# Weight conversions cut in halves and laid on half units, two of them taken into the opening steps, and the last weight's sums spread over ten units

## The chip, the cores and the metric

The kernel runs on one core of one Trainium2 chip. The metric is device microseconds of one execution; the time given for a kernel is the median of its runs. The engines are named as in the profile: PE (TensorE matmul), DVE (VectorE), ACT (ScalarE), POOL (GpSimd), SP (SyncE, which here issues nearly all DMAs).

## The reference, cut to what matters

Sparse attention, then two feed-forward blocks, all in float32, with float64 weights that the kernel turns into pairs of float32 parts on the chip.

```python
# q_l, k_l, v_l: 4 x 8 heads x 512 x 64 ; q_g, k_g, v_g: 4 x 8 x 32 x 64
s_g = scale * q_g @ [k_g, k_l]^T ;  out_g = softmax(s_g) @ [v_g, v_l]        # global rows
s_l = scale * q_l @ [k_g, k_l inside a window of 32 on both sides]^T
out_l = softmax(s_l) @ [v_g, v_l]
x = [out_g, out_l], heads side by side        # 2176 tokens x 512
h = x @ w_in                                  # 512 x 2048
g = where(h >= 1, h, where(h <= -1, 0, (h + 1)**2 / 4))
x = g @ w_out                                 # 2048 x 512
out = (x @ w_a * (x @ w_b)) @ w2_out          # 512 x 1536, 512 x 1536, 1536 x 512
```

## The kernel before

**Tiles and units.** Tokens are cut into six tiles (TILES), mostly of three blocks of 128 tokens, 384 columns wide. The first feed-forward block runs per tile in 16 units f, one for each slice of 128 of the 2048 hidden columns. A unit has two halves. The first (`h_unit`, kind 0) makes 12 matmuls into the PSUM tile hp (lines 593 to 595: each float32 product is three, high part by high, low by high, high by low); then ACT forms r (L921), DVE m (L922, L923), and one unit later ACT and DVE split m into g's high and low part (L926, L927). The second half (`x_unit`, kind 1) makes 12 matmuls of g of two units earlier (LAG) with w_out into four PSUM banks acc. PSUM tiles of tag "h" share four banks: hp, the attention's scores s, its transposes tp, its products o, ot.

**Order of the tiles.** `stages` says: tile 0's units 0 to 5, tile 1's 16 units, tile 0's units 6 to 15, then tiles 2 to 5. The attention of the next tile (its 12 items in 4 groups: s, masks L219, exps L227, transposes, o, os, ot) is cut into atoms that are dealt out between the halves. The attention of tile 0 itself runs before all this, in `begin()`, four steps k with filler matmuls (warm), whose order on each engine is fixed as written (`in_order`).

**Conversions.** The float64 weights of the first block come as 32 slices of 512 KB (i0, i1, o0, i2, o1, ...; `ws1`). Each is loaded to a raw tile (L102), and converted: ACT L110 reads the high words, DVE L111 and L112 put in the low words (`w_conv`), then ACT L119 and DVE L120 split the float32 into a high and a low part (`split`). The first ten raw tiles have buffers of their own; after that there are two (`sp["raw"]`), so a load waits until the L112 of two conversions earlier has read its tile. Before, i0 is converted in `begin()`'s steps 2 and 3, and i1 after the last step, followed by the masks and exps of tile 1's first group. Then a whole conversion at a time (`W1.step`) is issued ahead of a unit: in tile 0's units two a unit, in tile 1's one or two a unit until unit 12, each behind the newest L921 and L923 (`paced`).

**Second block.** Tiles go in three pairs (PAIRS) through 12 units of seven products (`ab_unit`, with y products L849 to L851). `side(u)` hangs other work on its places k: the next pair's sums (`x_pre`, L652 and L653) and splits (`x_op`), and during the second pair the sums of w2_out (`yw_sum`: four additions yq, L764 to L767; `yw_split`: two splits yo, L120), of which there are six. The third pair runs in `ab_step`.

The scheduler of the language layer decides the final order on each engine from the order in which the code issues, the dependencies and the `issue_after` edges; every engine then works its own list strictly in order.

Of the kernel before, what the change touches and what calls it, by code (L numbers as in the profile page):

```python
# [14 lines left out]
ALU = mybir.AluOpType  # L15
# [38 lines left out]
LEAD1 = 2  # L54
# [15 lines left out]
def body(tc, qk, vw, kg, vg, vt, w1i, w1o, w2a, w2b, w2o, mask, eye, out):  # L70
# [404 lines left out]
    pend = []  # L475
# [6 lines left out]
    def w_end():  # L482
        key, tf = pend.pop(0)
        w = slot()
        split(w[:, 0], w[:, 1], tf)
        wslots[key] = w

# [15 lines left out]
    def begin():  # L503
# [9 lines left out]
        for k in range(n):  # L513
# [5 lines left out]
            if k == n - 1:  # L519
                w_end()  # L520
            fill(FILLS[0])
            v_part(g[k])
            s_part(g[k + 2]) if k + 2 <= n else None
            g[k].v_post()
            if k + 2 < n:
                g[k + 2].mask()
            elif k + 2 == n:
                w_begin()
            fill(FILLS[1])
# [4 lines left out]
        w_begin()  # L534
        g[n].s_post()
# [361 lines left out]
    def paced(fn):  # L897

        with tc.issue_after(at["act"]), tc.issue_after(at["dve"]):
            return fn()  # L900

    def h_unit(t, f):
# [22 lines left out]
        def fin():  # L925
            nc.scalar.activation(gh[:, :W], m[:, :W], AF.Copy)  # L926
            nc.vector.tensor_tensor(gl[:, :W], m[:, :W], f32(gh[:, :W]), ALU.subtract)  # L927
# [41 lines left out]
    for u in range(len(units)):  # L969
        for kind in (0, 1):  # L970
            if kind == 0:
                if u >= len(units):
                    continue
                t, f = units[u]
                si = stage[u]
                if si == 0:
                    while f and W1.si < min(2 * f + LEAD1, n1):
                        paced(W1.step)
                if si == 1:
                    want = max(n1 + (len(ws1) - n1) * (f + 1) // (NF1 - 3), 2 * f + LEAD1 + 2)  # L980
                    while W1.si < min(want, len(ws1)):
                        paced(W1.step)
                if si == 1 and f == NF1 - 3:
# [64 lines left out]

    def side(u):
# [7 lines left out]
        def run(k):  # L1057
            if f == 1 and k == 0:
                x1_load(s + 1)
            if f == NF2 - 2 and k == 6:  # L1060
                behind(x_pre, s + 1)
# [11 lines left out]
            if s == 1:  # L1073
                c = f // 2
                if f % 2 == 0:
                    if k == 0 and f == 0:
                        yw_load(0)
                    elif k == 6:
                        behind(yw_sum, c)
                        if c < 5:  # L1080
                            yw_load(c + 1)
                elif k in (2, 5):
                    yw_split(c, k // 3)
# [256 lines left out]
```

## Time and profile before

| | |
|---|---|
| Runs of the kernel before | 897.07, 897.57, 901.92 us; median 897.57 us |
| The profiled execution's own time | 897.45 us |
| Its span in the profile | 895.6 us |
| PE busy | 874.0 us, 98% of the span |
| DVE busy | 621.0 us, 69% |
| ACT busy | 474.7 us, 53% |
| Granted TensorE clock, mean of the span | 0.994 |

The profile is of one execution. Its time is 1.85 us longer than its span, and 0.12 us below the median of the runs. A row of a timeline is "start us, duration us, engine, line, operation, out<-in, shape, count", and in square brackets how long the engine sat idle before it and what ended that. Durations of matmuls overlap: the step from one to the next is the rate. PEclk is the granted TensorE clock as a share of 2.4 GHz, so 1.00 is 2.4 GHz and a stretch wholly at 1.2 GHz reads 0.50.

### The profile page before, as it was taken

How to read it: one execution, taken by the hardware profiler on the slowest of the kernel's cores; microseconds unless marked ns; L12 is line 12 of the kernel's file. 1: busy time of each engine (PE TensorE's matmuls, PEld its weight loads, DVE VectorE, ACT ScalarE, POOL GpSimd, SP SyncE). 2: the span in 40 equal slices, each digit the busy share in tenths (PEclk: the TensorE clock that was granted, in tenths of full speed). 3: DMA queues.
4: the chain of work that ended last, by engine and by line, in shares of the span. 5: the costliest groups of instructions: out<-in, count | busy, mean ns of one | idle time of the engine just before them, and what ended most of it. 6: DMA issues, size and time to landing. Idle time of an engine off the chain costs nothing.

```text
span 895.6 us, 19345 instructions
## 1 busy us (share of the span) xinstructions
PE 874.0 (98%) x7394; PEld 822.9 (92%) x7394; DVE 621.0 (69%) x1524; ACT 474.7 (53%) x1151; POOL 0.3 (0%) x5
## 2 busy tenths in 40 slices
PE   7899989999999999999999999999999999999998
PEld 6688979999999999988999999999999998999998
DVE  4888887676556555555498687777977769776683
ACT  4787664555445444434465555555645556455442
POOL 0000000000000000000000000000000000000000
PEclk9999989999999999999999999999999999999999
DMA  9977664875344532444373455433486532644521
GB/s 312 387 216 241 211 220 140 277 228 187 119 149 139 165 135 89 137 127 133 118 241 113 150 171 165 164 118 121 135 303 220 188 129 91 198 140 130 192 110 53
DMA packets 77612, 153.60 MB, mean 172 GB/s; under 512 B 9296, under 2 KB 35792, under 8 KB 77520
## 3 DMA queue, kind: packets, MB, share of 16 engines
q1 hardware_dynamic: 76944, 151.85, 51.6%
q8 instruction: 58, 0.95, 0.4%
q10 hardware_dynamic: 576, 0.52, 0.2%
q14 instruction: 34, 0.28, 0.1%
HBM read 119.05 MB, written 33.29 MB: 170 GB/s over the span
## 4 chain that ended last, share of the span: by engine, by line
PE 83%; DMA 9%; DVE 4%; ACT 3%; issue 1%; SPq 1%; ACTq 0%; DVEq 0%
PE hp L593 6%; PE acc L593 6%; PE hp L595 6%; PE acc L594 6%; PE hp L594 6%; PE acc L595 6%; PE pb L785 4%; PE pb L783 4%; PE pb L786 4%; PE py L850 3%; PE py L851 3%; PE py L849 3%; PE px L783 3%; DMA wraw<-in_w1i_dram 3%; PE px L786 3%; PE px L785 3%
## 5 line engine op out<-in xcount | busy, mean ns | idle before, releaser
L593 PE MATMUL hp<-xh,w 128*128 128x384 f32 (+1 forms) x384 | 132.2, 344 | 4.4 <-DVE m L922 3.0
L593 PE MATMUL acc<-g,w 128*128 128x384 f32 (+1 forms) x384 | 127.8, 334 | 0.8 <-ACT w L119 0.8
L594 PE MATMUL hp<-xh,w 128*128 128x384 f32 (+1 forms) x384 | 127.2, 331 | 0.1
L595 PE MATMUL hp<-xl,w 128*128 128x384 f32 (+1 forms) x384 | 127.2, 332 | 0.0
L595 PE MATMUL acc<-g,w 128*128 128x384 f32 (+1 forms) x384 | 126.3, 329 | 0.0
L594 PE MATMUL acc<-g,w 128*128 128x384 f32 (+1 forms) x384 | 125.9, 328 | 0.0
L922 DVE SCALAR_TENSOR_TENSOR m<-hp,r 128x384 f32<-128x384 f32 (+1 forms) x96 | 51.2, 533 | 69.3 <-ACT r L921 68.5
L921 ACT ACTIVATE r<-hp,half 128x384 f32<-128x384 f32 (+1 forms) x96 | 53.8, 560 | 79.5 <-PE hp L595 78.6
L926 ACT ACTIVATE g<-m 128x384 fp32r<-128x384 f32 (+1 forms) x96 | 48.7, 507 | 61.3 <-DVE m L923 61.0
L593 PEld LDWEIGHTS hp<-xh,w 128*128 128x128 f32 x384 | 73.4, 191 | 6.9 <-DVE m L922 3.1
L783 PE MATMUL pb<-w 128*128 128x384 f32 (+1 forms) x240 | 78.1, 325 | 0.4 <-DVE m L827 0.2
L785 PE MATMUL pb<-w 128*128 128x384 f32 (+1 forms) x240 | 78.2, 326 | 0.0
L786 PE MATMUL pb<-w 128*128 128x384 f32 (+1 forms) x240 | 78.0, 325 | 0.0
L119 ACT ACTIVATE w<-wt 128x512 fp32r<-128x512 f32 (+1 forms) x94 | 53.2, 572 | 43.8 <-PE pb L786 30.6
L593 PEld LDWEIGHTS acc<-g,w 128*128 128x128 f32 x384 | 72.7, 190 | 2.0 <-ACT w L119 1.0
L595 PEld LDWEIGHTS hp<-xl,w 128*128 128x128 f32 x384 | 73.4, 191 | 1.0 <-DMA xl<-x0d 0.6
L594 PEld LDWEIGHTS hp<-xh,w 128*128 128x128 f32 x384 | 73.5, 191 | 0.7 <-DVE w L120 0.5
L595 PEld LDWEIGHTS acc<-g,w 128*128 128x128 f32 x384 | 72.6, 189 | 0.5 <-DVE g L927 0.2
L594 PEld LDWEIGHTS acc<-g,w 128*128 128x128 f32 x384 | 72.8, 190 | 0.1
L927 DVE TENSOR_TENSOR g<-m,g 128x384 fp32r<-128x384 f32 (+1 forms) x96 | 51.1, 533 | 23.0 <-ACT g L926 22.5
L227 ACT ACTIVATE e<-e,mn 128x128 f32<-128x128 f32 x128 | 48.0, 395 | 26.0 <-DVE os L261 22.6
L120 DVE TENSOR_TENSOR w<-wt,w 128x512 fp32r<-128x512 f32 (+1 forms) x94 | 57.5, 616 | 4.1 <-ACT w L119 3.1
(171 smaller groups left out, 2001.3 us busy)
## 6 DMA issues: line engine op xcount, KB each, us to landing
v<-in_vw_dram SPq DMA_DIRECT2D x64, 256.0 KB, 4.9
wt<-wd SPq DMA_DIRECT2D x50, 256.0 KB, 2.9
qk<-in_qk_dram SPq DMA_DIRECT2D x62, 176.0 KB, 4.5
wraw<-in_w1i_dram SPq DMA_DIRECT2D x16, 512.0 KB, 5.2
wraw<-in_w1o_dram SPq DMA_DIRECT2D x16, 512.0 KB, 4.1
wraw<-in_w2a_dram SPq DMA_DIRECT2D x12, 512.0 KB, 3.7
wraw<-in_w2b_dram SPq DMA_DIRECT2D x12, 512.0 KB, 3.7
wd<-wt SPq DMA_DIRECT2D x24, 256.0 KB, 2.2
```

Of the source, the lines that this page charges most:

```text
L119: nc.scalar.activation(hi, src, AF.Copy)
L120: nc.vector.tensor_tensor(lo, src, f32(hi), ALU.subtract)
L593: nc.tensor.matmul(acc, whi, xhi, start=first, stop=False)
L594: nc.tensor.matmul(acc, wlo, xhi, start=False, stop=False)
L595: nc.tensor.matmul(acc, whi, xlo, start=False, stop=last)
L783: nc.tensor.matmul(out[:, :n], w[:, 0, r], hi[:, c, :n], start=start and c == 0, stop=False, skip_group_check=True)
L785: nc.tensor.matmul(out[:, :n], w[:, 1, r], hi[:, c, :n], start=False, stop=False, skip_group_check=True)
L786: nc.tensor.matmul(out[:, :n], w[:, 0, r], lo[:, c, :n], start=False, stop=k in (1, 5, 6) and c == 1, skip_group_check=True)
L921: at["act"] = nc.scalar.activation(r[:, :W], hp[:, :W], AF.Relu, bias=half, scale=0.5 / W_UP).ins
L922: nc.vector.scalar_tensor_tensor(m[:, :W], hp[:, :W], 1.0 / W_UP, r[:, :W], ALU.mult, ALU.max)
L926: nc.scalar.activation(gh[:, :W], m[:, :W], AF.Copy)
L927: nc.vector.tensor_tensor(gl[:, :W], m[:, :W], f32(gh[:, :W]), ALU.subtract)
```

## The change

Four things, in the order of the diff. (1) `begin()`: i0's conversion begins in step 1 and ends (its split) in step 2; i1's begins in step 3; the masks of group 4, tile 1's first, move into step 2 and its exps into step 3. i1's split stays last, and the masks and exps that stood ahead of it are gone from there. (2) A conversion has two halves, `w_begin` (L110 to L112) and `w_end` (the split). `conv_to` is called at each half unit, ends as many conversions as are due there, and then begins one more. In tile 0's units one conversion is due for each half unit, in tile 1's the remaining 19 are spread over 30 half units, to unit 14. The edges of `paced` now follow g's split too. The pool for the second block's raw weights opens at tile 1's unit 15 and not at 13. (3) `x_pre` is called one unit earlier. (4) w2_out's sums and splits go to 18 places spread evenly over the second pair's units 0 to 9; before they had units 0 to 11, two units for each.

```diff
@@ -472,7 +471,7 @@
                 turn.o_turn()
         return run
 
-    pend = []
+    pend, ended = [], [0]
 
     def w_begin():
         pend.append(w_conv())
@@ -484,6 +483,7 @@
         w = slot()
         split(w[:, 0], w[:, 1], tf)
         wslots[key] = w
+        ended[0] += 1
 
     @contextlib.contextmanager
     def in_order():
@@ -516,23 +516,25 @@
             if k + 1 < n:
                 g[k + 1].exp()
             g[k].recip()
-            if k == n - 1:
-                w_end()
             fill(FILLS[0])
             v_part(g[k])
-            s_part(g[k + 2]) if k + 2 <= n else None
+            if k + 2 <= n:
+                s_part(g[k + 2])
             g[k].v_post()
-            if k + 2 < n:
+            if k + 2 <= n:
                 g[k + 2].mask()
-            elif k + 2 == n:
+            if k == n - 3:
                 w_begin()
+            elif k == n - 2:
+                w_end()
+            elif k == n - 1:
+                w_begin()
+                g[n].exp()
             fill(FILLS[1])
             g[k].o_turn()
             x_chunk(0, k, widths(0))()
             if k + 1 < n:
                 fill(FILLS[2])
-        w_begin()
-        g[n].s_post()
         w_end()
 
     atoms = [piece(START_GROUPS + 1, None)]
@@ -896,8 +898,18 @@
 
     def paced(fn):
 
+        if not at:
+            return fn()
         with tc.issue_after(at["act"]), tc.issue_after(at["dve"]):
             return fn()
+
+    def conv_to(n):
+        while ended[0] < n:
+            if not pend:
+                paced(w_begin)
+            paced(w_end)
+        if not pend and ended[0] < len(ws1):
+            paced(w_begin)
 
     def h_unit(t, f):
         W = widths(t)
@@ -923,8 +935,8 @@
         at["dve"] = nc.vector.scalar_tensor_tensor(m[:, :W], r[:, :W], 1.0, m[:, :W], ALU.min, ALU.mult).ins
 
         def fin():
-            nc.scalar.activation(gh[:, :W], m[:, :W], AF.Copy)
-            nc.vector.tensor_tensor(gl[:, :W], m[:, :W], f32(gh[:, :W]), ALU.subtract)
+            at["act"] = nc.scalar.activation(gh[:, :W], m[:, :W], AF.Copy).ins
+            at["dve"] = nc.vector.tensor_tensor(gl[:, :W], m[:, :W], f32(gh[:, :W]), ALU.subtract).ins
         deferred.append(fin)
         gq[(t, f)] = (gh, gl)
 
@@ -968,19 +980,15 @@
     LAG = 2
     for u in range(len(units)):
         for kind in (0, 1):
+            t, f = units[u]
+            si = stage[u]
+            slot_n = 2 * f + kind
+            if si == 0:
+                conv_to(min(slot_n + 1, n1))
+            elif si == 1:
+                conv_to(min(n1 - (-(len(ws1) - n1) * (slot_n + 1) // (2 * NF1 - 2)), len(ws1)))
             if kind == 0:
-                if u >= len(units):
-                    continue
-                t, f = units[u]
-                si = stage[u]
-                if si == 0:
-                    while f and W1.si < min(2 * f + LEAD1, n1):
-                        paced(W1.step)
-                if si == 1:
-                    want = max(n1 + (len(ws1) - n1) * (f + 1) // (NF1 - 3), 2 * f + LEAD1 + 2)
-                    while W1.si < min(want, len(ws1)):
-                        paced(W1.step)
-                if si == 1 and f == NF1 - 3:
+                if si == 1 and f == NF1 - 1:
                     es_st.close()
                     sp["p"] = es_st.enter_context(tc.tile_pool(name="pc", bufs=1, reuse_waits="tile"))
                     sp["raw"], sp["wt"] = 2, 2
@@ -1046,6 +1054,11 @@
             while att_step(ends[goal[si]]):
                 pass
 
+    yw_at = {}
+    for i in range(18):
+        f, k = divmod(10 + 11 * i, 21)
+        yw_at.setdefault((f, (2, 4, 6)[k // 7]), []).append((i % 3, i // 3))
+
     def side(u):
         s, f = divmod(u, NF2)
 
@@ -1057,7 +1070,7 @@
         def run(k):
             if f == 1 and k == 0:
                 x1_load(s + 1)
-            if f == NF2 - 2 and k == 6:
+            if f == NF2 - 3 and k == 6:
                 behind(x_pre, s + 1)
             if f == NF2 - 1:
                 x_op(s + 1, k)
@@ -1071,16 +1084,15 @@
             if k == 4 and s == 0:
                 y_prep(f)
             if s == 1:
-                c = f // 2
-                if f % 2 == 0:
-                    if k == 0 and f == 0:
-                        yw_load(0)
-                    elif k == 6:
+                for kind, c in yw_at.get((f, k), ()):
+                    if kind == 0:
                         behind(yw_sum, c)
                         if c < 5:
                             yw_load(c + 1)
-                elif k in (2, 5):
-                    yw_split(c, k // 3)
+                    else:
+                        yw_split(c, kind - 1)
+            if s == 1 and f == 0 and k == 0:
+                yw_load(0)
         return run
 
     def fill0(k):
```

The final orders show what that moves. On ACT, at the end of `begin()` (wt_704, then wt_702, is i1's conversion; e_708, then e_628, are the exps of tile 1's first group; xh3 is the last chunk of tile 0's x; r_739, then r_743, is unit 0's first step), before:

```order
L119 ACTIVATE w_660<-wt_624 128x512
L373 ACTIVATE xh3_700<-ot_696 128x384
L110 ACTIVATE wt_704<-wraw0_209 128x512
L227 ACTIVATE e_708,sm_710<-e_708,mn_709 128x128 x6
L119 ACTIVATE w_723<-wt_704 128x512
L921 ACTIVATE r_739<-hp_726,half_73 128x384
```

and now:

```order
L109 ACTIVATE wt_702<-wraw0_209 128x512
L226 ACTIVATE e_628,sm_630<-e_628,mn_629 128x128 x6
L109 ACTIVATE wt_726<-wraw0_223 128x512
L372 ACTIVATE xh3_719<-ot_715 128x384
L118 ACTIVATE w_723<-wt_702 128x512
L933 ACTIVATE r_743<-hp_730,half_73 128x384
```

i1's first step and the six exps now stand ahead of xh3, and the first step of o0 (wt_726) too; the exps no longer stand between i1's two steps.

On ACT, in tile 1's units (wt is the first step of a conversion, which waits for the raw tile's load; w the high part of its split; r and g belong to units; xraw and pt to the attention), before:

```order
L110 ACTIVATE wt_1822<-wraw_1769 128x512
L921 ACTIVATE r_1844<-hp_1831,half_73 128x384
L119 ACTIVATE w_1826<-wt_1822 128x512
L110 ACTIVATE wt_1864<-wraw_1778 128x512
L926 ACTIVATE g_1846<-m_1845 128x384
L921 ACTIVATE r_1895<-hp_1882,half_73 128x384
L246 ACTIVATE pt_1908<-tp_1905 128x256
L119 ACTIVATE w_1868<-wt_1864 128x512
L110 ACTIVATE wt_1873<-wraw_1829 128x512
L278 ACTIVATE xraw0_1702<-ot_1910 128x384
L926 ACTIVATE g_1897<-m_1896 128x384
L110 ACTIVATE wt_1929<-wraw_1871 128x512
```

and now:

```order
L933 ACTIVATE r_1892<-hp_1879,half_73 128x384
L245 ACTIVATE pt_1905<-tp_1902 128x256
L277 ACTIVATE xraw0_1708<-ot_1907 128x384
L938 ACTIVATE g_1894<-m_1893 128x384
L118 ACTIVATE w_1926<-wt_1873 128x512
L109 ACTIVATE wt_1929<-wraw_1854 128x512
L933 ACTIVATE r_1948<-hp_1935,half_73 128x384
L118 ACTIVATE w_1954<-wt_1929 128x512
L109 ACTIVATE wt_1957<-wraw_1877 128x512
L938 ACTIVATE g_1950<-m_1949 128x384
L245 ACTIVATE pt_1984<-tp_1981 128x256
L933 ACTIVATE r_1999<-hp_1986,half_73 128x384
```

Before, a conversion's first step and its split follow each other with at most a unit's r between, and two first steps come close together; now each split is followed at once by the first step of the next conversion, with about one conversion for each r.

On DVE, where the second pair ends (t10 to t21 are `x_pre`'s, yq the last of w2_out's sums, m and w the unit's own), before:

```order
L652 TENSOR_TENSOR t10_9488<-x1r10_8515,x1r00_8507 128x384
L652 TENSOR_TENSOR t11_9492<-x1r11_8517,x1r01_8509 128x384
L653 TENSOR_TENSOR t20_9489<-x1r12_8519,t10_9488 128x384
L653 TENSOR_TENSOR t21_9493<-x1r13_8521,t11_9492 128x384
L764 TENSOR_TENSOR yq_9502<-yin_9300 128x256
L766 TENSOR_TENSOR yq_9502<-yin_9300 128x256
L765 TENSOR_TENSOR yq_9502<-yq_9502,yin_9300 128x256
L120 TENSOR_TENSOR w_6562<-x1r01_8509,w_6561 128x384
L767 TENSOR_TENSOR yq_9502<-yin_9300,yq_9502 128x256
```

and now:

```order
L654 TENSOR_TENSOR t10_9409<-x1r10_8515,x1r00_8507 128x384
L654 TENSOR_TENSOR t11_9413<-x1r11_8517,x1r01_8509 128x384
L655 TENSOR_TENSOR t20_9410<-x1r12_8519,t10_9409 128x384
L655 TENSOR_TENSOR t21_9414<-x1r13_8521,t11_9413 128x384
L814 TENSOR_TENSOR m_9429<-px_6974,r_9426 128x320
L119 TENSOR_TENSOR w_6436<-wt_9509,w_6436 128x512
L119 TENSOR_TENSOR w_6439<-wsum_9513,w_6439 128x512
L825 TENSOR_TENSOR m_9430<-px_6974,r_9428 128x320
L119 TENSOR_TENSOR w_6479<-wsum_9513,w_6479 128x256
```

The yq rows that followed `x_pre` have gone to earlier units, and `x_pre` is followed by the weight splits of a unit that comes one earlier.

## Rows read from the trace of the kernel before

**Rows 1.** The page's first part: busy time and share of the span.

```profile
PE 874.0 (98%) x7394; PEld 822.9 (92%) x7394; DVE 621.0 (69%) x1524; ACT 474.7 (53%) x1151; POOL 0.3 (0%) x5
```

**Rows 2.** Waits of PE over the whole span: us in total, times, longest.

```profile
PE tp L244 <- ACT pt L246: 1.3, 1, 1.3
...
PE py L783 <- ACT r L1142: 1.0, 1, 1.0
PE px L783 <- DVE m L823: 0.8, 1, 0.8
```

**Rows 3.** Stretches: PE, PEld, DVE, ACT, POOL busy, then granted clock, DMA share, GB/s.

```profile
35.50:41.50 6.00, 5.17 (x20) 4.50 (x21) 6.00 (x21) 6.00 (x21) 0.00 (x0) 0.72 1.03 398
65.50:73.50 8.00, 6.42 (x122) 5.15 (x122) 7.57 (x30) 7.26 (x24) 0.00 (x0) 1.00 0.87 281
119.80:131.00 11.20, 7.00 (x67) 6.84 (x68) 9.72 (x29) 6.83 (x20) 0.00 (x0) 0.70 0.72 218
750.00:760.00 10.00, 8.97 (x45) 7.13 (x44) 9.93 (x22) 5.73 (x15) 0.00 (x0) 1.00 0.52 184
```

**Rows 4.** Timeline of PE, tile 0's units 0 to 2.

```profile
33.36 0.86 PE L204 MATMUL s<-qk 64*32 64x128 f32 x38 [0.72 <-DVE mn L219]
35.49 0.69 PE L593 MATMUL hp<-xh,w 128*128 128x384 f32 x1 [1.27 <-ACT w L119]
...
39.46 0.60 PE L244 MATMUL tp<-ident,e 128*128 128x128 f32 x4
40.81 0.96 PE L593 MATMUL acc<-g,w 128*128 128x384 f32 x4 [0.76 <-ACT w L119]
```

**Rows 5.** Timeline of DVE, the opening steps.

```profile
21.49 0.56 DVE L376 TENSOR_TENSOR xl<-ot,xh 128x384 fp32r<-128x384 f32 x1 [3.10 <-ACT xh L373]
```

**Rows 6.** Timeline of ACT, the last opening step and behind it.

```profile
27.45 0.64 ACT L119 ACTIVATE w<-wt 128x512 fp32r<-128x512 f32 x1
...
32.49 0.40 ACT L227 ACTIVATE e<-e,mn 128x128 f32<-128x128 f32 x1 [1.43 <-DVE mn L219]
...
34.82 0.62 ACT L119 ACTIVATE w<-wt 128x512 fp32r<-128x512 f32 x1
```

**Rows 7.** Timeline of PE, tile 1's units 8 to 11.

```profile
110.16 0.42 PE L593 MATMUL hp<-xh,w 128*128 128x384 f32 x1
...
121.05 0.88 PE L254 MATMUL o<-v,pt 128*32 128x64 f32 x48 [1.25 <-DVE m L922]
124.88 0.69 PE L593 MATMUL hp<-xh,w 128*128 128x384 f32 x1 [2.95 <-DVE m L922]
...
131.97 0.33 PE L593 MATMUL hp<-xh,w 128*128 128x384 f32 x1
...
134.05 0.38 PE L244 MATMUL tp<-ident,e 128*128 128x128 f32 x2
```

**Rows 8.** Timeline of ACT, tile 1's unit 8.

```profile
118.06 0.67 ACT L110 ACTIVATE wt<-wraw 128x512 f32<-128x512 f32 x1 [1.81 <-DMA wraw<-in_w1i_dram]
118.64 0.57 ACT L921 ACTIVATE r<-hp,half 128x384 f32<-128x384 f32 x1
```

**Rows 9.** Waits of ACT from 84 to 119 us.

```profile
ACT wt L110 <- DMA wraw<-in_w1i_dram: 6.2, 5, 1.8
ACT wt L110 <- DMA wraw<-in_w1o_dram: 3.8, 3, 2.5
```

**Rows 10.** Waits of the SP queue from 0 to 180 us.

```profile
SPq L102 <- DVE wt L112: 44.7, 21, 6.6
```

**Rows 11.** The raw tiles: us from issue to landing, min, median, max.

```profile
DMA to landing us min/median/max: 3.4/4.1/8.7
```

**Rows 12.** Timeline of DVE, the same conversion as rows 8.

```profile
119.23 0.69 DVE L112 SCALAR_TENSOR_TENSOR wt<-wraw,wt 128x512 int32<-128x512 int32 x1
```

**Rows 13.** Timeline of DVE, the end of the second pair.

```profile
743.96 1.02 DVE L652 TENSOR_TENSOR t<-x1r,x1r 128x384 f32<-128x384 f32 x2
...
745.83 0.42 DVE L764 TENSOR_TENSOR yq<-yin 128x256 f32<-128x256 f32 x1
```

More of the change, by code (lines that the diff above doesn't have):

```diff
@@ L53 @@
 FA = 6
-LEAD1 = 2
 PAIRS = [(0, 1), (4, 5), (2, 3)]
```

## The prediction, made before the changed kernel ran

> **What bounds the kernel now.** The page's first part comes first: PE is busy 98% of the span [rows 1], so an edit pays only where PE stands still or runs slowly, and the question is where the missing 2% lie. The waits of PE answer that next. They name few places, all before 160 us or after 740 us; between 160 and 740 us no wait is listed, and what moves there moves for nothing. The stretches [rows 3] then show the two places where PE also ran slowly: from 35.5 to 41.5 us the granted clock is 0.72 and from 119.8 to 131.0 us 0.70, while it is 1.00 from 65.5 to 73.5 us although PE idles 1.58 of 8.00 us there. Last come the timelines of PE, DVE and ACT around these places.
>
> Place A, tile 0's first units [rows 4]. PE waits 0.72 us for tile 1's first masks, which free the banks of the next scores; 1.27 us for i1's split; 0.76 us for o0's. Between the second and the third wait a unit's 12 matmuls take 39.46 - 35.49 = 3.97 us. A unit at 2.4 GHz takes 134.05 - 131.97 = 2.08 us [rows 7], so the half clock costs 1.89 us. Sum 0.72 + 1.27 + 0.76 + 1.89 = 4.64 us. The chain behind it is plain: the six exps begin at 32.49 us, when the first mask is there, and i1's split stands behind them on ACT, at 34.82 us [rows 6].
>
> Place B, 65.5 to 73.5 us: 1.58 us idle [rows 3], of which a wait for ACT's pt of 1.3 us is most [rows 2]. ACT comes late there as in C.
>
> Place C, tile 1's units 8 to 10. PE waits 1.25 and 2.95 us for DVE's m [rows 7]. m needs ACT's r, and r is badly late: unit 8's matmuls begin at 110.16 us and end 2.1 us later, its r starts at 118.64 us [rows 7, 8]. So for some 6 us of work PE ran ahead of ACT, until the four banks were full. Why ACT fell behind is its own waits: from 84 to 119 us its conversions' first steps wait 10.0 us for raw tiles, eight times [rows 9], the last 1.81 us directly ahead of that r [rows 8]. And the loads are late because SP waits for DVE's L112 to free a raw tile, 44.7 us in 21 waits [rows 10]. After the waits the 24 matmuls up to 131.97 us take 7.09 us where two units at 2.4 GHz take 4.16, so 2.93 us go to the half clock. Sum 1.25 + 2.95 + 2.93 = 7.13 us.
>
> Place D, the end of the second pair and what follows. DVE is busy 9.93 of 10.00 us from 750 to 760 us [rows 3]; PE waits 0.8 us for its m and, later, 1.0 us for ACT's r [rows 2].
>
> **The change part by part.** No arithmetic is added or removed; it all moves.
>
> *The opening steps (A).* Three things leave the stretch behind the opening steps: six masks, six exps, and i1's first three instructions. In step 2 the masks go where DVE did i0's L111 and L112, and these go into step 1, where DVE idles 3.10 us behind them [rows 5]; I cost both at nothing. Were i0's load late, ACT would wait with step 1's xh behind it, and the 3.10 us cover that too; what goes beyond them would be lost. In step 3 there is a price: i1's first step (0.67 us [rows 8]), the exps (34.82 - 32.49 = 2.33 us [rows 6]) and o0's first step (0.67 us) now stand on ACT ahead of xh3. ACT is through with step 3's pt at 27.45 us, where i0's split began [rows 6]; then the exps run from 28.1 to 30.4, xh3 ends at about 31.4 us and xl3 at about 32.0, and unit 0's last matmul waits for it some 0.3 us. The scores of the next group then find their banks free and run at 32.2 us, and unit 1, whose split is done at 32.6, at 33.1 us instead of 35.49, with the clock up as PE has hardly paused. It ends at 35.2 instead of 39.46 us: 4.3 us ahead.
>
> Behind that the half-unit order puts new waits, as each split now comes half a unit before its use and DVE is full. Following DVE's and ACT's new lists with the durations of before, I find 0.65 us for a bank that the next masks free, 0.85 us for i2's split, and 0.9 us for i3's, which stands behind masks and os: 2.4 us, in place of the 0.76 us of before. 4.3 - 2.4 + 0.76 = 2.7 us. The lists carried on to unit 1's last acc would have it 4.0 us ahead, but that leaves out what PE loses at every change of tile. **A = 3.0**, nearer to the first; bounds 0.1 (the clock falls once more, at the 2.93 us of C) to 4.64.
>
> A rule of the Trainium skill speaks against this part. The trace has the half clock behind 0.72 + 1.27 us of waits and behind 1.25 + 2.95 us, but none in 1.58 us of idling spread over 8 us [rows 3, 4, 7]. The Trainium skill's page "TensorE: Matmul & The Clock Gate", section "HAM oscillation — how this bites in real kernels", says that a wait between short bursts of matmuls lets the clock gate fall back, and the next burst starts cold each time. By the row of 65.5 us my three waits, 2.4 us over 13, keep the clock, and A stays 3.0; by the rule it would fall once more, at the 1.89 us of rows 4, and A would be 1.1.
>
> *Tile 0's later units (B).* With the raw tiles freed about 3 us sooner the loads of conversions 10 to 13 go out sooner by as much, and ACT's waits there shrink. Between 0 and 1.58 us; **B = 0.9**, a bit over half, as DVE is still nearly full.
>
> *Tile 1's units (C).* Two raw tiles make a loop: first step, L111 and L112 (119.92 - 118.06 = 1.9 us from ACT's start to a free tile [rows 8, 12]), then a landing of 4.1 us in the median [rows 11]: 6.0 us for two conversions, 3.0 us each. A unit's 24 matmuls take 4.16 us, with the attention's a little more. Before, 19 conversions fell on 13 units, 13 x 4.16 / 19 = 2.85 us each: no room, and they came in pairs. Now 19 fall on 15 units, 3.28 us each, evenly: two take 6.56 us, so that a landing of up to 4.7 us is hidden. A later one holds ACT by the difference, and the 0.3 us of room in each conversion takes it back before the banks are full. So r keeps up and all of 7.13 us can go. I leave 0.8 us for landings above the median and for the second block's first raw loads, which now start later, close to the loads of tile 0's x. **C = 6.3**, bounds 3 (a smaller backlog that still empties PE once, with half the price) to 7.13.
>
> *w2_out's sums and x_pre (D).* From 744 to 757 us DVE loses four sums t (two rows of 1.02 us), four yq (4 x 0.42) [rows 13] and two splits yo, over 3.7 us of 13, to units in which PE waits for nobody. That ends the 0.8 us and the small waits around it. The later 1.0 us hangs on loads behind stores, which I leave as it is. **D = 1.0**, bounds 0 to 2.0.
>
> **Sum.** 3.0 + 0.9 + 6.3 + 1.0 = 11.2 us. The profiled execution took 897.45 us, 1.85 more than its span and 0.12 below the median; 897.45 - 11.2 = 886.25, **886.3 us**.
>
> **The rivals.**
>
> *R1, ACT stays behind in tile 1.* If r is late because DVE and ACT have too much to do in these units and not because of loads, spreading helps only a little. For it: DVE is busy 9.72 of 11.20 us at the place [rows 3]. Against it: the 10.0 us that ACT stood waiting [rows 9] exceed the 6 us by which r was late. C is then 0 to 1: 897.45 - 4.9 - 0.5 = 892 us.
>
> *R2, the start gives its gain back.* DVE is the limit in tile 0's units, the splits come just before their use, and the waits grow or the clock falls again. For it: DVE and ACT are busy 6.00 of 6.00 us from 35.5 us [rows 3]. A and B are 0.1 and 0: 897.45 - 7.4 = 890 us.
>
> *R3, slower.* Each split is now followed at once by the next first step, which sits at the head of ACT's list until its raw tile has landed, and every r, exp and pt waits behind it. It decides once landings average over 4.7 us. At 7 us (8.7 has occurred [rows 11]) the loop is 8.9 us for two conversions, 4.45 each: 19 x 4.45 = 84.6 us for matmuls of 15 x 4.16 = 62.4, so up to 22.2 us of stall instead of 7.13, and 897.45 - 4.9 + 15.1 = 908 us; it is slower than before from landings of about 5.9 us on. Against it: the median of 4.1, and fewer loads per time than before.
>
> *R4, no change that can be told.* PE's waits only move and each is met by another: 894 to 900 us. Against it: two of the waits are tied to instructions that are gone from the place.
>
> **How the numbers follow.** The forecast 0.65, R1 0.13, R2 0.12, R3 0.04, R4 0.06. The forecast's own range is 882.1 to 890: all four bounds at their best, 4.64 + 1.58 + 7.13 + 2.0 = 15.35, give 882.1, and A and C each short by 1.9 give 890. The range to hold 8 in 10 takes R1 and R2 in at the top: 881.5 to 892.0. About 0.5% (4.5 us) is what a measurement of this kernel can tell from no change. Faster by more takes the forecast, nearly all of R1 and R2: 0.87. Within: R4 and a rest: 0.08. Slower: R3 and a rest: 0.05.
>
> **What would show it.** Right: no hp unit of tile 0 or 1 at half clock, the second one at about 33 us; from 84 to 119 us ACT's waits for raw tiles under 3 us in sum, and each r within 2 us of its matmuls; no PE wait over 1 us in tile 1; no wait for m near 750 us. Wrong: a stretch at 1.2 GHz in tile 0's units (R2), an r over 4 us late in units 8 to 10 (R1), waits of 2 us and more for raw tiles ahead of each r (R3), new waits between 160 and 740 us.

## The result, and the profile after

The changed kernel takes 889.17 us in the median of 4 runs (886.22 to 889.73), the kernel before 898.63 us (897.07 to 901.92); the ratio is 0.9883, with a 95% interval of 0.9846 to 0.992. The forecast was 886.3 us, with 881.5 to 892.0. The profiled execution took 886.22 us, 11.23 us less than that of before; the sum of the forecast was 11.2. Part of this agreement is luck: by the medians the gain is 9.46 us, and both profiles of the changed kernel are of its fastest executions (886.22 and 885.94 us). The terms do not agree so well. To compare them the span is cut at rows that both kernels have. Timeline of PE, kernel before; in the order of the rows: the scores that end A, the wait that ends B, the scores that open tile 2 and end C (the first hp, at 29.74 us, begins A).

```profile
53.05 0.94 PE L204 MATMUL s<-qk 64*32 64x128 f32 x48
...
73.66 0.44 PE L244 MATMUL tp<-ident,e 128*128 128x128 f32 x2 [1.34 <-ACT pt L246]
...
153.92 0.94 PE L204 MATMUL s<-qk 64*32 64x128 f32 x48
```

The same places in the changed kernel, with the first hp ahead of them (its lines are one lower up to about line 480, two higher from about 540 and eight to thirteen, mostly twelve, higher from about 900; in the experiments they move by a few lines more).

```profile
30.55 0.42 PE L595 MATMUL hp<-xh,w 128*128 128x384 f32 x1
...
50.99 0.94 PE L203 MATMUL s<-qk 64*32 64x128 f32 x48
...
71.59 0.44 PE L243 MATMUL tp<-ident,e 128*128 128x128 f32 x2 [0.84 <-ACT pt L245]
...
145.27 0.94 PE L203 MATMUL s<-qk 64*32 64x128 f32 x48
```

The first block's last r starts at 496.31 us before and at 489.44 us after. The differences of these starts give the ledger (us; the second profile is that of the experiment e1_again):

| stretch | before | changed | changed, second profile | forecast |
|---|---|---|---|---|
| start to the first hp | 29.74 | 30.55 | 30.07 | no term |
| A, to the scores | 23.31 | 20.44 | 20.52 | -3.0 |
| B, to tile 1's first tp | 20.61 | 20.60 | 20.72 | -0.9 |
| C, to tile 2's first scores | 80.26 | 73.68 | 73.85 | -6.3 |
| E, to the first block's last r | 342.39 | 344.17 | 344.17 | no term |
| D, from there to the end | 399.29 | 394.96 | 394.77 | -1.0 |

A (-2.87) and C (-6.58) came as forecast, B gave nothing, D gave 4.33 where 1.0 was forecast, and two stretches without a term cost 0.81 and 1.78. The total is right because D's excess of 3.3 pays for the other three, 0.9 + 0.8 + 1.8; that they cancel is luck.

Stretches of the changed kernel, which answer to [rows 3] (us busy of PE, PEld, DVE, ACT, POOL, then granted clock, DMA share, GB/s):

```profile
17.00:30.00 13.00, 10.74 (x230) 8.99 (x214) 9.18 (x38) 7.55 (x24) 0.00 (x0) 0.87 1.01 376
30.00:41.50 11.50, 10.34 (x101) 8.07 (x100) 10.56 (x33) 10.39 (x36) 0.00 (x0) 1.00 1.04 397
65.50:73.50 8.00, 5.88 (x121) 4.63 (x120) 6.96 (x26) 7.89 (x27) 0.00 (x0) 1.00 0.84 258
119.80:131.00 11.20, 11.20 (x67) 11.17 (x66) 9.07 (x29) 8.09 (x24) 0.00 (x0) 1.00 0.57 202
741.00:751.00 10.00, 10.00 (x54) 8.99 (x53) 9.96 (x25) 6.36 (x16) 0.00 (x0) 1.00 0.39 119
```

The half clock is gone from tile 0's first units (0.72 before) and from 120 to 131 us (0.70 before, and PE now busy 11.20 of 11.20). PE is also busy through the end of the second pair, though DVE there is as full as before (9.96 of 10.00, against 9.93). In 65.5 to 73.5 us PE is busy less than before, 5.88 against 6.42, though the same work lies some 2 us earlier here; over B itself PE is busy 17.91 of 20.60 us, before 18.14 of 20.61.

### The profile page after: what moved, and what is told of

It is laid out like the page before. It is cut to its first block, busy times and chain, and to the rows that moved or that the text cites. A ratio compares the mean times of both kernels' runs of the same rounds, so it can differ in the third digit from the quotient of the medians.

```text
span 884.4 us, 19341 instructions
## 1 busy us (share of the span) xinstructions
PE 871.8 (99%) x7394; PEld 821.6 (93%) x7394; DVE 624.3 (71%) x1524; ACT 472.1 (53%) x1151; POOL 0.3 (0%) x5
## 4 chain that ended last, share of the span: by engine, by line
PE 83%; DMA 6%; ACT 5%; DVE 4%; issue 1%; SPq 1%; ACTq 0%; DVEq 0%
PE hp L595 6%; PE acc L595 6%; PE acc L597 6%; PE acc L596 6%; PE hp L597 6%; PE hp L596 6%; PE pb L787 4%; PE pb L785 4%; PE pb L788 4%; PE py L852 3%; PE py L853 3%; PE py L851 3%; PE px L785 3%; PE px L787 3%; PE px L788 3%; ACT e L226 2%
## 5 line engine op out<-in xcount | busy, mean ns | idle before, releaser
L595 PEld LDWEIGHTS hp<-xh,w 128*128 128x128 f32 x384 | 72.3, 188 | 6.7 <-ACT xh L372 1.7
L596 PEld LDWEIGHTS hp<-xh,w 128*128 128x128 f32 x384 | 72.5, 189 | 0.2 <-DVE w L119 0.2
L226 ACT ACTIVATE e<-e,mn 128x128 f32<-128x128 f32 x128 | 47.8, 393 | 24.8 <-DVE os L260 21.9
```

Of the source, the lines that this page charges most:

```text
L226: nc.scalar.activation(self.e[:, n, h], self.e[:, n, h], AF.Exp, bias=self.mn[:, n, h:h + 1], scale=-1.0, accum_out=acc)
L595: nc.tensor.matmul(acc, whi, xhi, start=first, stop=False)
L596: nc.tensor.matmul(acc, wlo, xhi, start=False, stop=False)
```

## The experiments

Each stretch in each experiment's profile, cut at the same rows (us; B and C together, as their border moves with single loads). Times and ratios are those of repeated runs beside the kernel before, with the 95% interval.

| run | first hp | A | B + C | E | D | median | ratio to before |
|---|---|---|---|---|---|---|---|
| before | 29.74 | 23.31 | 100.87 | 342.39 | 399.29 | 898.4 to 900.3 | 1 |
| e1_again | 30.07 | 20.52 | 94.57 | 344.17 | 394.77 | 888.91 | 0.9885 [0.9859, 0.9911] |
| e2_begin | 31.65 | 20.49 | 100.56 | 341.60 | 399.30 | 896.86 | 0.9975 [0.996, 0.9991] |
| e3_deep | 30.04 | 23.67 | 93.88 | 342.45 | 399.06 | 890.77 | 0.9907 [0.9882, 0.9932] |
| e4_d | 30.45 | 24.08 | 100.41 | 341.91 | 395.55 | 894.15 | 0.995 [0.9927, 0.9972] |
| e5_whole15 | 30.85 | 23.42 | 95.77 | 346.68 | 399.78 | 897.73 | 0.9982 [0.9966, 0.9997] |
| e6_halves13 | 31.37 | 19.93 | 96.89 | 343.39 | 395.02 | 888.07 | 0.9874 [0.9854, 0.9893] |
| e7_deep_after | 32.35 | 20.28 | 93.12 | 343.20 | 395.25 | 883.77 | 0.9831 [0.981, 0.9852] |
| e8_no_halves | 31.07 | 21.46 | 93.19 | 341.48 | 396.60 | 885.18 | 0.9837 [0.9811, 0.9863] |
| e9_yw | 32.94 | 23.35 | 98.81 | 342.25 | 396.95 | 897.09 | 0.9984 [0.9967, 1.0002] |
| e10_xpre | 31.74 | 23.26 | 99.83 | 342.01 | 397.56 | 896.10 | 0.9976 [0.996, 0.9993] |
| e11_mixed4 | 29.98 | 20.42 | 94.44 | 343.06 | 395.80 | 885.05 | 0.9844 [0.9822, 0.9867] |
| e12_mixed3 | 32.00 | 20.32 | 93.57 | 343.24 | 394.67 | 885.21 | 0.9848 [0.9825, 0.987] |

How far a stretch moves by itself is read from the kernels that have no edit in it: A 23.26 to 24.08 us (before, e4, e5, e9, e10), B + C 98.81 to 100.87 (before, e4, e9, e10), E 341.60 to 342.39 (before, e2, e4, e9, e10), D 399.06 to 399.78 (before, e2, e3, e5). C alone moves by 2.2 us among the four (78.07 to 80.26). Each is one profile, so smaller differences of a stretch show nothing by themselves, and the kernel before stands at the upper end in B + C.

**e1_again**: no edit.

> The changed kernel once more, for a second profile and a better interval. Its four times lie between 886.2 and 889.7 us with granted clocks of 0.994 to 0.998. Theory: the stretches A, C and D give the same gains again (20.4 us from the first hp to the scores at 50.99 us, 73.7 us from tile 1's first tp to tile 2's first scores, and 395.0 us from the last r of the first block to the end, each within 0.4 us), and what differs between runs lies in the opening steps before the first hp or at tile 2's start. Rival: C is a matter of luck, and then this profile shows an r over 4 us late in tile 1's units 8 to 10 and C at 76 us or more. Time 886 to 890 us.

A, C, E and D repeat within 0.2 us, so the ledger is no matter of one execution. The rival is out: C is 73.85 us, though r still comes late here (4.70 and 6.02 us after the first matmul of units 9 and 10).

**e2_begin**: the kernel before with the changed `begin()`.

```
-            if k == n - 1:
-                w_end()
...
+            if k == n - 3:
+                w_begin()
+            elif k == n - 2:
+                w_end()
+            elif k == n - 1:
+                w_begin()
+                g[n].exp()
```

> The kernel before with the opening steps of the changed one, and nothing else. If term A is all the opening steps' own: from the first hp to the scores at 53.05 us 20.4 us instead of 23.3 (-2.9), C and D as before, 895 us. Rival, that the half-unit conversions share in A: -1.0 to -2.0 in A. Rival, that the start moves the load loop ahead too: C moves by more than 1 us.

A is 20.49 us: all of the term (-2.82) is the opening steps' own. C moved by 1.7 us (78.61), but B by 1.34 the other way; together they are 0.3 under the kernel before, so no shift of the load loop shows. The rows show why A can be the same with whole conversions: one wait in place of three. Timeline of PE, e2_begin.

```profile
34.95 0.44 PE L595 MATMUL hp<-xh,w 128*128 128x384 f32 x1
...
39.43 0.79 PE L595 MATMUL acc<-g,w 128*128 128x384 f32 x3 [1.63 <-ACT w L119]
```

**e3_deep**: the load loop opened, everything else as before.

```
-        if len(wraws) < EARLY.count("w"):
-            raw = wp.tile(..., name="wraw0", tag="w", bufs=32)
+        if not wraws:
+            raws.extend(wp.tile(..., name="wraw0", tag="w", bufs=32) for _ in range(31))
+        if len(wraws) < len(raws):
+            raw = raws[len(wraws)]
...
-        W1.load_to(W1.si + sp["raw"])
+        W1.load_to(W1.si + 4)
```

> The kernel before, but its first 31 raw tiles lie in the weights' 32 slots (each slot is free until its weight is split), four loads ahead instead of two, so that no load waits for a raw tile to be freed; conversions stay whole, two at a time, in the same 13 units. Theory that the load loop of two raw tiles is the cause in C: ACT's 10.0 us of waits for raw tiles between 84 and 119 us shrink to under 2, the 7.1 us of C go, and B's 1.6 us in part: 888 to 890 us. Rival, that ACT and DVE have too much to do in units 0 to 12: ACT's waits for raw tiles go but r of units 8 to 10 stays over 4 us late, C stays at 79 us or more, 896 us.

B + C is 93.88 us, 6.99 less than before and 4.9 less than the lowest of the kernels without an edit there, with conversions whole and in their old places: as much as the changed kernel's halves and spread brought (6.3 to 6.6). Waits of ACT, e3_deep, 84 to 119 us, beside [rows 9]:

```profile
ACT w L121 <- DVE wt L114: 4.4, 7, 1.1
ACT g L928 <- DVE m L925: 2.9, 5, 1.0
ACT e L229 <- DVE mn L221: 0.7, 1, 0.7
ACT r L923 <- PE hp L597: 0.6, 1, 0.6
```

No wait for a raw tile is left, ACT at one point even waits for PE, and PE has no listed wait from 75 us to the end of tile 1. DVE is busy 34.03 of 35.00 us there, so the rival (too much to do) had its best chance and did not show. The loop of two raw tiles is the cause of what C lost.

**e4_d**: `side()` and `yw_at` of the changed kernel alone.

> The kernel before with w2_out's sums in ten units and x_pre one unit earlier, and nothing else: the place D alone. In the profile of the changed kernel 4.1 us came from here instead of the 1.0 forecast (the pauses between PE's starts sum to 4.12 us from 735 to 792 us before, 0.18 after). If D stands by itself, the stretch from the last r of the first block to the end takes 395.0 us instead of 399.3, 893.5 us. Rival, that D hangs on what the first block does: 1 us or less, 896.5 us.

D is 395.55, so 3.74 us are its own and the rival is out. Whether the rest of the 4.33 needs the whole change is not shown: among the kernels that have this edit D lies between 394.67 (e12) and 396.60 us (e8).

**e5_whole15**: the room without the halves.

```
-                    want = max(n1 + (len(ws1) - n1) * (f + 1) // (NF1 - 3), 2 * f + LEAD1 + 2)
+                    want = max(n1 + (len(ws1) - n1) * (f + 1) // (NF1 - 1), 0)
...
-                if si == 1 and f == NF1 - 3:
+                if si == 1 and f == NF1 - 1:
```

> The kernel before with tile 1's 19 conversions spread over 15 units instead of 13, but whole, ahead of a unit, one or two at a time; two raw tiles as before. Theory that the room is what counts (3.28 us a conversion against a loop of 3.0): from tile 1's first tp to tile 2's first scores 74 to 75.5 us instead of 80.3, 891 us or a little under. Rival, that the halves do it (one conversion at a time between two half units, so that no pair waits twice): 78.5 us or more here, 896 us or more.

Tile 1's part did what the theory said (C is 72.97 us from 77.07 on, PE without a wait), and the time did not: 897.73 us where 891 was expected. What the theory left out stands at tile 2's start. Timelines of SP, of ACT and of PE there, e5_whole15.

```profile
147.82 0.33 SPq L102 DMA_DIRECT2D wraw<-in_w2a_dram  x1
```

```profile
151.42 0.67 ACT L110 ACTIVATE wt<-wraw 128x512 f32<-128x512 f32 x1 [1.07 <-DMA wraw<-in_w2a_dram]
```

```profile
154.94 0.41 PE L593 MATMUL hp<-xh,w 128*128 128x384 f32 x1 [3.16 <-DVE mn L219]
```

The second block's first raw load goes out at 147.82 us, as its pool opens only when tile 1's last conversion is done. ACT waits for it, DVE's L111 for ACT, the masks mn stand behind that, and PE waits for them 3.16 us. E costs 4.3 us more than before, and B 2.2 more in this profile.

**e6_halves13**: the halves without the room.

```
-                ... (slot_n + 1) // (2 * NF1 - 2)), len(ws1)))
+                ... (slot_n + 1) // (2 * NF1 - 6)), len(ws1)))
```

> The changed kernel, but tile 1's 19 conversions end after 13 units as before, still in halves on half units. Theory that the room counts: 2.85 us a conversion is under the loop's 3.0, so the backlog of r builds up again and the stretch from tile 1's first tp to tile 2's first scores takes 77 us or more instead of 73.7, 892 us. Rival, that the halves do it: 74.5 us or less, 889 us.

C is 75.95 us (from 72.24 to 148.19), between the two expectations. The backlog does build up: beside 0.69 us for masks at 96.70, one wait for m is left of the two of before, 1.67 us where 1.25 and 2.95 were. Timeline of PE, e6_halves13.

```profile
121.96 0.44 PE L595 MATMUL hp<-xh,w 128*128 128x384 f32 x1 [1.67 <-DVE m L934]
```

But it is not the load loop that builds it: from 84 to 119 us ACT waits 3.2 us for raw tiles, less than the 5.4 us of the changed kernel, and 6.0 us for DVE's L111 where that has 3.5. By the profiles the halves alone are worth 4.3 us in C and the room 2.3 more, of which tile 2's start takes 0.8 back; 2.3 is about the scatter of C, and in time the two kernels can't be told apart.

**e7_deep_after**: the changed kernel with the edit of e3_deep.

> The changed kernel with the first 31 raw tiles in the weights' slots, four loads ahead. In its profile ACT waits 1.69 us for a raw tile at 62.3 us, and the exps, r and pt that PE then waits for stand behind it. If that is why B gave nothing: the stretch from the scores at 50.99 us to tile 1's first tp shrinks from 20.6 to 19 us or less, tile 1 keeps its 73.7 us or gains a few tenths, and tile 2's start (its first xh loads stood behind two raw loads on SP) gains up to 0.6: 886 us where the changed kernel has 889. Rival, that ACT and DVE are simply full in B, or that the further loads take DMA from the scores' operands: no gain, 888.5 to 891 us.

It beats both kernels: 0.9831 [0.981, 0.9852], the changed kernel 0.9885 [0.9859, 0.9911]. But B did not come: 52.63 to 72.97 us is 20.34. ACT waits for no raw tile any more from 54 to 119 us, and another wait has taken the place. Waits of PE, e7_deep_after, 54 to 80 us.

```profile
PE s L205 <- DMA qk<-in_qk_dram: 1.3, 1, 1.3
PE tp L245 <- ACT pt L247: 0.6, 2, 0.3
```

Against the two profiles of the changed kernel it is 1.2 to 1.5 us shorter in B + C and 1.0 in E.

**e8_no_halves**: e3_deep with the new opening steps and D, conversions whole.

> The kernel before with the new opening steps, w2_out's sums and x_pre as in the changed one, and the raw tiles in the weights' slots, four ahead; the conversions stay whole, in the old places. If halves and spread do nothing but cover the load loop: -2.8 at the start, -7.0 from there to tile 2 and -3.9 at the end of the second pair, span 882 us, 885 to 888 us, not slower than the changed kernel. If the halves bring something of their own: over 890 us.

885.18 us, and B + C within 0.1 us of e7's. With the loop open the halves and the spread are worth nothing in B + C and in the time that these runs can tell. The other stretches differ, though: against e7, A is 1.18 us longer, D 1.35 longer and E 1.72 shorter. In A PE has the one long wait of e2_begin, and behind it the granted clock falls. Timeline of PE and a stretch (as above), e8_no_halves.

```profile
38.84 1.40 PE L597 MATMUL acc<-g,w 128*128 128x384 f32 x4 [1.62 <-ACT w L121]
```

```profile
38.00:43.00 5.00, 4.16 (x27) 3.35 (x28) 4.89 (x10) 4.59 (x12) 0.00 (x0) 0.66 0.81 308
```

In e2_begin the same wait, 1.63 us, left the clock at 1.00 through A. In the six profiles with tile 0's conversions in halves (the changed kernel twice, e6, e7, e11, e12) it is 1.00 through A as well, with A at 19.93 to 20.52 us; whether the halves ensure that, one fall in two profiles with the new opening steps and whole conversions doesn't show.

**e9_yw** and **e10_xpre**: the two parts of D, each alone.

```
+            if s == 1:
+                for kind, c in yw_at.get((f, k), ()):     # e9_yw
...
-            if f == NF2 - 2 and k == 6:
+            if f == NF2 - 3 and k == 6:                   # e10_xpre
```

> The kernel before with w2_out's sums in ten units, x_pre where it was. The place D gave 3.7 us with both parts. DVE's load there (from 744 us four sums t at 1.02 us a pair, four yq of 0.42, two yo splits) is 2.0 us of t against 3.0 of yq and yo. Theory that DVE's load in sum counts: about half of the gain each, the stretch from the last r of the first block to the end 397 to 398 us instead of 399.3. Rival, that only what stands last ahead of m counts (the yo splits and yq): 395.5 to 396.5, all of the gain.

> The kernel before with x_pre one unit earlier, w2_out's sums where they were. By DVE's load in sum: 397 to 398 us for the stretch from the last r of the first block to the end, and with e9 the two halves add up to the 3.7 us of both. If only the sums of w2_out count: 399 us, no gain.

D is 396.95 and 397.56: 2.34 and 1.73 us, which add up to 4.1 (3.7 for both in e4_d). Each part gains by itself, and the sums of w2_out alone do not gain all, so the rivals fall and the theory of DVE's load in sum fits, with 396.95 a little outside its range. The shares are rough, as e8 with both parts has 396.60. How the load becomes waits is not shown: in its fullest 10 us DVE is as busy in the changed kernel as before. The whole-run ratios of these two (intervals to 1.0002 and 0.9993) are too coarse to show any of it.

**e11_mixed4**, **e12_mixed3**: e7 with tile 1's conversions whole, in 13 units, the second block's pool opened at unit 13 again, four and three loads ahead.

```
-                conv_to(min(n1 - (-(len(ws1) - n1) * (slot_n + 1) // (2 * NF1 - 2)), len(ws1)))
+                if kind == 0:
+                    conv_to(min(max(n1 + (len(ws1) - n1) * (f + 1) // (NF1 - 3), 2 * f + 4), len(ws1)), False)
```

> Changed kernel with 31 raw tiles in the weights' slots, four loads ahead (as e7), and tile 1's conversions whole, in 13 units as before, tile 0's still in halves. With late conversions at tile 1's end e7 and the changed kernel lost time at tile 2's start (from tile 2's first scores to the first block's last r 343.2 and 344.2 us, against 342.4 before and 341.5 in e8). If that is from conversions that stand beside tile 2's first masks and splits: 341.5 here, span from the first hp on 1.6 us shorter than e7's 851.9, 882.5 us. Rival, that halves in tile 1 are needed: C over 74 us, 885 us or more.

> As e11, but three loads ahead instead of four. In e7 and e8 PE waited 1.3 to 1.4 us near 62 us for the operands of the scores, whose load stands behind the raw loads. If the fourth load ahead is what delays them: that wait is under 0.5 us and the time 1 us under e11's. Rival, that it doesn't depend on the depth, or that the wait for raw tiles comes back: the same as e11 or up to 2 us slower.

E stays at 343.06 and 343.24 us, so the theory of late conversions falls; C is 73.40 and 73.41 us, so its rival, that halves in tile 1 are needed, falls too. With three loads ahead the wait for the scores' operands near 62 us is 0.81 us instead of 1.29, not under 0.5, with 0.40 for v beside it; the time is the same.

## Why the prediction was right, and where it was not

**A, right in sum (3.0 forecast, 2.87), with two errors.** Timeline of PE, the changed kernel; it answers to [rows 4].

```profile
32.72 0.45 PE L595 MATMUL hp<-xh,w 128*128 128x384 f32 x1 [0.35 <-ACT xh L372]
34.55 0.44 PE L595 MATMUL hp<-xh,w 128*128 128x384 f32 x1
37.44 0.41 PE L243 MATMUL tp<-ident,e 128*128 128x128 f32 x2 [0.32 <-DVE mn L218]
40.48 0.44 PE L595 MATMUL hp<-xh,w 128*128 128x384 f32 x1 [0.45 <-ACT w L118]
```

The price of 0.3 us ahead of unit 0's last matmuls is there as forecast (0.35). The second unit begins 4.00 us after the first, where 3.36 was forecast and 5.75 was before: less ahead than thought. The new waits behind it are 0.32 and 0.45 us where 0.65, 0.85 and 0.9 were forecast: following the lists with the durations of before gave waits that were too long. The clock stays at 1.00 from 30 to 41.5 us in both profiles of the changed kernel, so A did not come out at the 1.1 us of one more fall of the clock; but the last two waits, 0.77 us in sum, were a third of the 2.4 forecast, so this does not test whether 2.4 us would have brought it down. That e8's clock fell in this stretch behind 1.62 us, and e2's did not behind 1.63, leaves open what decides. The case in the Trainium skill's page "TensorE: Matmul & The Clock Gate", section "HAM oscillation — how this bites in real kernels", has waits of some 3 to 5 us between the bursts, so the prediction's rule went beyond it for waits of 0.65 to 0.9 us.

**B, wrong (0.9 forecast, 0.01).** The step that failed is that the loads of conversions 10 to 13 go out about 3 us sooner "and ACT's waits there shrink". The loads went out 3.6, 0.8, 2.5 and 2.9 us sooner, and ACT waited 2.1 us for raw tiles in this stretch where it had waited 1.8. The load that gained only 0.8 us (57.59 us, before 58.40) is the one ACT then waits longest for. Timeline of ACT, the changed kernel.

```profile
59.52 0.69 ACT L109 ACTIVATE wt<-wraw 128x512 f32<-128x512 f32 x1 [0.37 <-DMA wraw<-in_w1o_dram]
...
62.31 0.66 ACT L109 ACTIVATE wt<-wraw 128x512 f32<-128x512 f32 x1 [1.69 <-DMA wraw<-in_w1i_dram]
...
66.13 0.56 ACT L933 ACTIVATE r<-hp,half 128x384 f32<-128x384 f32 x1
66.59 0.63 ACT L245 ACTIVATE pt<-tp 128x256 f32<-128x256 f32 x2
```

The next conversion's first step, issued right behind the last split, holds ACT 1.69 us for its raw tile; six exps, r and pt stand behind it, and PE waits 0.75 us for that pt at 67.01 us. That is the mechanism of R3, at one place and for 2 us. e7 shows that even this is not the whole: without it the scores' operands come late.

**C, right in size (6.3 forecast, 6.58); the cause of the loss before is shown** by e3_deep: the loop. Units 8 and 10 in the changed kernel, timelines of PE and then of ACT; they answer to [rows 7, 8].

```profile
108.44 0.42 PE L595 MATMUL hp<-xh,w 128*128 128x384 f32 x1
...
119.02 0.45 PE L595 MATMUL hp<-xh,w 128*128 128x384 f32 x1 [0.31 <-DVE m L934]
```

```profile
111.14 0.55 ACT L933 ACTIVATE r<-hp,half 128x384 f32<-128x384 f32 x1
...
125.05 0.56 ACT L933 ACTIVATE r<-hp,half 128x384 f32<-128x384 f32 x1
```

In unit 8 r starts 2.70 us after its unit's first matmul, where it was 8.48; in units 9, 10 and 11 it starts 4.42, 6.03 and 5.01 us after (before 8.65, 7.22 and 4.03), and PE waits 0.31 us for m in unit 10. So "r keeps up" was too much: the backlog got small enough that PE hardly stops, and it missed the prediction's own sign of each r within 2 us of its matmuls, which take 2.1 us. With the loop open as well (e7) units 9 and 10 have 2.46 and 4.17. The reason given for the gain, that 3.28 us of room exceed the loop's 3.0, was at most half: e5 and e6 show that room without halves wins C and loses it again at tile 2's start, and that halves without room win two thirds, as far as single profiles can tell. And ACT's waits for raw tiles from 84 to 119 us were forecast under 3 us; they are these, with a longest of 2.0:

```profile
ACT wt L109 <- DMA wraw<-in_w1o_dram: 4.6, 3, 2.0
...
ACT wt L109 <- DMA wraw<-in_w1i_dram: 0.8, 2, 0.5
```

They still stop ACT for 5.4 us, half of before, in five places instead of eight.

**D, the mechanism right and the size wrong (1.0 forecast, bounds 0 to 2.0; 4.33).** The failed step was to take the listed waits for the whole loss: "That ends the 0.8 us and the small waits around it", and "the later 1.0 us hangs on loads behind stores, which I leave as it is". Timeline of PE, the kernel before, around the listed wait of 0.81 us.

```profile
750.80 0.39 PE L851 MATMUL py<-w,g 128*128 128x512 f32 x1
752.00 0.42 PE L783 MATMUL px<-w,w 128*128 128x320 f32 x1 [0.81 <-DVE m L823]
752.25 0.31 PE L785 MATMUL px<-w,w 128*128 128x320 f32 x1
752.40 0.31 PE L786 MATMUL px<-w,w 128*128 128x320 f32 x1
...
752.83 0.31 PE L786 MATMUL px<-w,w 128*128 128x320 f32 x1
753.33 0.44 PE L783 MATMUL pb<-w 128*128 128x384 f32 x1 [0.18 <-DVE m L827]
```

Undisturbed, the next start follows a matmul of 512 columns after 0.23 us and one of 320 after 0.15. Here it follows after 1.20, then 0.25 instead of 0.15, and after 0.50: a listed wait of 0.81 costs 0.97 + 0.10, and one of 0.18 costs 0.35 + 0.11. Other pauses of 0.3 us are not listed at all. Added up so from 735 to 792 us, PE lost 4.12 us before, 1.12 in e4_d and 0.18 in the changed kernel: that is 3.94 of the 4.33. The late 1.0 us went too; in e4_d, e8 and e9 a wait of 0.6 to 0.7 us for ACT's r is left in the last third. The prediction put it down to loads behind stores. Timelines of SP, the kernel before, then the changed one.

```profile
726.86 24.09 SPq L774 DMA_DIRECT2D wyd<-yo  x3
754.24 0.32 SPq L1114 DMA_DIRECT2D t<-wqd  x1
```

```profile
742.51 0.80 SPq L1126 DMA_DIRECT2D t<-wqd  x2
```

Before, a store of yo waits 22.2 us at the head of the queue for DVE's split, with the last third's first load behind it. But once the store is out, at 750.95 us, that load waits 3.2 us more for a weight split of DVE. In the changed kernel no store stands there, the load itself waits 25.4 us for such a split, and it goes out 4.9 us sooner, counted from the first block's last r. So the first load hangs on DVE in both kernels; how the 1.0 us, some 30 us later, hangs on it is not shown.

**Left out: E (+1.78).** From tile 2's scores on, 1.0 us goes by the second hp unit, 0.5 in the first unit of tile 2 and 0.3 in that of tile 3. The first: timelines of SP and then of PE, the changed kernel.

```profile
141.76 0.33 SPq L101 DMA_DIRECT2D wraw<-in_w2b_dram  x1
142.18 0.39 SPq L582 DMA_DIRECT2D xh<-x0d  x1
```

```profile
148.41 0.44 PE L595 MATMUL hp<-xh,w 128*128 128x384 f32 x1 [0.67 <-DMA xh<-x0d]
```

The reload of tile 0's xh goes out 1.16 us after the last hp unit began (141.02), before it was 0.54: the second block's raw loads, which now go out later, stand ahead of it. The prediction had named this neighbourhood, inside C's 0.8 us, and not as a term. The later 0.8 us are seen as well: timelines of ACT and then of PE, the changed kernel, tile 2's first unit.

```profile
195.56 0.66 ACT L109 ACTIVATE wt<-wraw 128x512 f32<-128x512 f32 x1
196.12 0.51 ACT L372 ACTIVATE xh<-xraw 128x384 fp32r<-128x384 f32 x1
```

```profile
196.69 0.45 PE L595 MATMUL hp<-xh,w 128*128 128x384 f32 x1 [0.28 <-ACT xh L372]
```

A first step of the second block's conversions now stands ahead of the last xh, and PE waits for that. In the kernel before it stands earlier. The first units of tiles 2 and 3 take 5.0 and 4.8 us in every kernel with tile 0's conversions on half units (the changed one, e6, e7, e11, e12) and 4.5 in all others, e8 among them. The order may come from `fin()` setting the point behind which these conversions are issued; that was not tried and stays open.

Of the rivals, R1 and R2 are out (r is late, but C has its gain; the start keeps its own), and R3 is real but small.

## What to carry to other kernels

A wait that several places share is worth taking away at its source first: here four loads ahead into buffers that stand empty anyway did as much in B + C as rearranging all conversions, and with the loads ahead the rearrangement brought nothing more there. Price a stall by the starts around it less their undisturbed pitch, not by the wait that is listed: the difference was a factor of two here. When a total agrees, cut the span at shared rows and look whether the terms do.

## What the runs showed that was not expected

The first hp begins between 29.74 and 32.94 us in the 14 profiles, with no visible relation to the edits; this 3.2 us may be much of the scatter in the times (885.94 to 892.79 us for the changed kernel alone), which is not shown, as the slower executions have no profile. Two pauses of PE stand there, and the one tends to replace the other: "issue" before a warming matmul, and the scores' operands that land at 23.2 to 24.8 us whenever PE gets there early. Timeline of PE, the kernel before, then the changed one.

```profile
20.22 0.38 PE L189 MATMUL warm<-ident 128*128 128x128 f32 x1 [2.70 <-issue]
...
23.61 1.36 PE L204 MATMUL s<-qk 64*32 64x128 f32 x48 [0.33 <-DMA qk<-in_qk_dram]
```

```profile
18.65 0.38 PE L188 MATMUL warm<-ident 128*128 128x128 f32 x1 [0.53 <-issue]
...
23.44 1.56 PE L203 MATMUL s<-qk 64*32 64x128 f32 x48 [1.73 <-DMA qk<-in_qk_dram]
```

What the issue pause is (0.5 to 3.6 us) no run here tells. After the 1.73 us the clock was at its lower level, 1.2 GHz, for a while (0.87 over 17 to 30 us); in e1_again, after 1.20 us at the same place, it was not (1.00). In 11 of the 14 profiles it was at that level for some time in these 13 us, which adds to the scatter of the first hp.
